# Linear attention with decay, then an MLP, on one core: the recurrence in chunks of 64 steps on column halves of the array instead of chunks of 128 on the whole array

## The chip, the cores and the metric

The kernel runs on one core of one Trainium2 chip. The metric is device time in microseconds (us) of one execution; lower is better. All arithmetic is in float32. The engines are called as in the profile: PE is TensorE's matmul, PEld its weight load, DVE is VectorE, ACT is ScalarE, POOL is GpSimd, SP is SyncE (here it only issues DMAs).

## What is computed

The reference is a recurrence over 768 steps for each of 4 batches and 8 heads, with 48 columns per head, followed by layer norm and a two-layer MLP with a residual:

```python
for t in range(S):
    kt, vt, rt, wt = (k[:, :, t], v[:, :, t], r[:, :, t], w[:, :, t])
    cur = np.einsum('bhd,bhe->bhde', u[None] * kt, vt)
    y[:, :, t] = np.einsum('bhd,bhde->bhe', rt, state + cur)
    state = wt[:, :, :, None] * state + np.einsum('bhd,bhe->bhde', kt, vt)
...
xn = (x - mu) / np.sqrt(var + 1e-06) * g_ln     # x: (4, 768, 384), the 8 heads side by side
ch = np.maximum(xn @ w_ch1, 0.0) @ w_ch2        # 384 -> 1536 -> 384
return x + ch
```

Here w lies between 0.8 and 0.95. The two MLP weights arrive as float64 and are converted to float32 on the chip.

## The kernel before

**Units.** A unit is one batch and one pair of heads, so there are 16 units, 4 to a batch. The two heads of a unit lie on 128 partitions, 64 each, of which 48 are used. The recurrence runs in 6 chunks of 128 steps. Inside a chunk the weight of step s in a later step t is a product of r, k and all decays between them; it is split by levels. At level `lev` the block size is n = 1, 2, .. 64, and an entry A[s, t] belongs to the level at which s lies in the left and t in the right of two sibling blocks. K and R are multiplied, level by level, by the products T of whole blocks of decays, so that A = K . R holds at each level.

**A level of a unit** (`levels`, 7 of them): PE makes 6 matmuls into two PSUM tiles of three chunks (line 269), with 128 columns of K as the stationary operand and 128 moving columns (two heads of 64). R is kept padded, as [128 partitions, 2 heads, 768], with zeros where the other head's partitions are, so that one matmul serves both heads. DVE copies the entries of this level out of PSUM through a mask, one copy for each three chunks (line 281); at the last level ACT does it (line 278). POOL multiplies K in place (line 282), and DVE multiplies R in place, one instruction per head on 64 partitions (line 293). K is read by this level's matmuls before POOL may change it, and R before DVE may.

**The rest of a unit.** `prep` turns w, k and r with PE transposes (line 210), copies them out with ACT (216, 220), makes the products T on POOL (232), and the step's own term on POOL and DVE (238 to 249). `tail` turns K back (310), makes the state that each chunk adds (`kv`, 5 matmuls, line 315), masks it (318), runs the recurrence over chunks on DVE (323, 325), and forms the output y from A and v (338) and from the carried state (343), which DVE adds into x (347).

**A matmul and its instructions.** A float32 matmul is two pairs of weight load and matmul on the chip: 672 matmuls at line 269 are 1344 instructions in the profile. A transpose is one pair.

**The MLP** (`mlp`) of a batch goes in two groups of 384 tokens: statistics and normalising on DVE, 9 transposes (381), 36 matmuls `h_ps` for the hidden layer (390), 36 `o_ps` for the output (400). It needs all four units of its batch.

**Order.** Python generators interleave one step of unit q's levels, the end of unit q - 1, the start of unit q + 1, one part of the weight conversion (24 parts, one per level step), and as many MLP steps of the batch before as keep pace. A scheduler in the framework then fixes each engine's order, so that an instruction can stand somewhat later or earlier than it was written. Each engine runs its own list in that order.

Of the kernel before, what the change touches and what calls it, by code (L numbers as in the profile page):

```python
# [28 lines left out]
def kernel(  # L29
# [26 lines left out]
    TT = 3                # token tiles that go through the MLP together  # L56
    RN = TT * P
    NG = NC // TT
    assert D <= HP and NC % CB == 0 and DM % P == 0 and DF % P == 0
# [3 lines left out]
    p3 = ctx.enter_context(tc.tile_pool(name="p3", bufs=3))  # L63
    ph = ctx.enter_context(tc.tile_pool(name="ph", bufs=14))
# [6 lines left out]
    NU = len(units)  # L71

    # a head's D columns lie in HP, the rest of which stays zero
# [4 lines left out]
    vs, xs = {}, {}  # L78
# [10 lines left out]
    def load_v(q):  # L89
        b, g = units[q]  # L90
        if g == 0:
            vs[b] = p2.tile([P, NC, H, D], F32, tag="v", name=f"v{b}")
        for h in (2 * g, 2 * g + 1):
            SP.dma_start(
                out=vs[b][:, :, h, :], in_=v[b, h].rearrange("(c p) d -> p c d", p=P)
            )

# [1 line left out]
    for nm in "wkr":  # L99
        for t in nat[nm]:  # L100
            POOL.memset(t[:, :, :, D:HP], 0.0)
# [372 lines left out]
```

## Time and profile before

| what | us |
|---|---|
| three runs | 804.66, 800.58, 804.47 (median 804.47) |
| span of the profiled execution, first to last instruction | 798.1 |
| PE busy | 704.1 (88%) |
| PEld busy | 527.0 (66%) |
| DVE busy | 457.0 (57%) |
| POOL busy | 258.8 (32%) |
| ACT busy | 191.5 (24%) |
| DMA, mean over the span | 42 GB/s |

The profiled execution shows its span only; what the runs' median has beyond it is 804.47 - 798.1 = 6.4 us. Busy time is the union of an engine's instructions; PE instructions overlap their neighbours' ends, so the pace of PE is read from the distance between starts and not from the duration of one. PEclk is the clock granted to TensorE, in tenths of full speed. In a group of instructions "128\*64" is the part of the array that is used, rows by columns; then come the output and input sizes.

### The profile page before, as it was taken

How to read it: one execution, taken by the hardware profiler on the slowest of the kernel's cores; microseconds unless marked ns; L12 is line 12 of the kernel's file. 1: busy time of each engine (PE TensorE's matmuls, PEld its weight loads, DVE VectorE, ACT ScalarE, POOL GpSimd, SP SyncE). 2: the span in 40 equal slices, each digit the busy share in tenths (PEclk: the TensorE clock that was granted, in tenths of full speed). 3: DMA queues.
4: the chain of work that ended last, by engine and by line, in shares of the span. 5: the costliest groups of instructions: out<-in, count | busy, mean ns of one | idle time of the engine just before them, and what ended most of it. 6: DMA issues, size and time to landing. Idle time of an engine off the chain costs nothing.

```text
span 798.1 us, 9669 instructions
## 1 busy us (share of the span) xinstructions
PE 704.1 (88%) x3640; PEld 527.0 (66%) x3640; DVE 457.0 (57%) x791; ACT 191.5 (24%) x402; POOL 258.8 (32%) x329
## 2 busy tenths in 40 slices
PE   4446665677699999999999999999999999999998
PEld 3346565567577767776867777777777776655554
DVE  5699999988964656485645555686444643200000
ACT  3034151503223122321322032212230212020110
POOL 8646564554532314141423333333121110000000
PEclk9558585859999999999999999999999999999999
DMA  9667241402310102023202020110000000000000
GB/s 155 102 139 154 64 120 60 119 5 46 75 30 16 41 20 46 0 55 70 56 1 46 21 55 1 30 35 11 1 1 11 20 1 1 20 11 11 20 1 30
DMA packets 107855, 33.86 MB, mean 42 GB/s; under 512 B 101536, under 2 KB 104736, under 8 KB 107808
## 3 DMA queue, kind: packets, MB, share of 16 engines
q1 hardware_dynamic: 107808, 33.24, 19.7%
q8 instruction: 29, 0.48, 0.2%
q14 instruction: 18, 0.15, 0.1%
HBM read 28.51 MB, written 4.72 MB: 42 GB/s over the span
## 4 chain that ended last, share of the span: by engine, by line
PE 76%; DVE 15%; POOL 3%; issue 3%; ACT 1%; DMA 1%; SPq 1%; POOLq 0%; ACTq 0%; DVEq 0%
PE h_ps L390 24%; PE o_ps L400 23%; PE a_ps L269 18%; DVE R L293 5%; PE y L338 4%; DVE A L281 3%; PE y L343 2%; POOL tot L232 2%; PE kv L315 1%; DVE we L184 1%; DVE wm L188 1%; PE k_ps L210 1%; DVE we L176 1%; PE r_ps L210 1%; DVE wm L192 1%
## 5 line engine op out<-in xcount | busy, mean ns | idle before, releaser
L269 PE MATMUL a_ps<-R,kT 128*128 128x128 f32 (+1 forms) x1344 | 198.5, 304 | 75.2 <-DVE R L293 64.5
L269 PEld LDWEIGHTS a_ps<-R,kT 128*128 128x128 f32 (+1 forms) x1344 | 186.2, 206 | 106.2 <-issue 44.1
L281 DVE COPY_PREDICATED A<-mask,a_ps 128x384 f32<-128x384 int8 x192 | 135.2, 730 | 139.1 <-PE a_ps L269 133.0
L390 PE MATMUL h_ps<-xT,w_sb 128*128 128x384 f32 x576 | 195.3, 489 | 0.5 <-ACT xT L382 0.5
L400 PE MATMUL o_ps<-w_sb,h 128*128 128x384 f32 x576 | 193.1, 487 | 0.0
L282 POOL TENSOR_TENSOR kT<-kT,tot 128x384 f32<-128x384 f32 x96 | 92.0, 958 | 257.4 <-PE a_ps L269 257.4
L400 PEld LDWEIGHTS o_ps<-w_sb,h 128*128 128x128 f32 x576 | 106.5, 190 | 67.1 <-issue 0.9
L390 PEld LDWEIGHTS h_ps<-xT,w_sb 128*128 128x128 f32 x576 | 105.6, 190 | 65.6 <-ACT xT L382 1.7
L293 DVE TENSOR_TENSOR R<-R,tot 64x384 f32<-64x384 f32 x160 | 133.4, 833 | 2.2
L406 DVE TENSOR_TENSOR o<-o_ps,x 128x384 f32<-128x384 f32 x24 | 13.4, 557 | 156.6 <-PE o_ps L400 156.6
L395 ACT ACTIVATE h<-h_ps 128x384 f32<-128x384 f32 x96 | 47.0, 490 | 149.1 <-PE h_ps L390 149.0
L338 PE MATMUL y<-v,A 128*128 128x48 f32 x384 | 56.0, 278 | 0.0
L338 PEld LDWEIGHTS y<-v,A 128*128 128x128 f32 x384 | 54.0, 207 | 0.5
L220 ACT COPY R<-r_ps 64x384 f32<-64x384 f32 x64 | 30.2, 472 | 55.3 <-PE r_ps L210 54.2
L292 ACT COPY rs<-R 64x384 f32<-64x384 f32 x32 | 16.3, 509 | 108.4 <-DVE R L293 107.9
L238 POOL TENSOR_TENSOR rk<-nat_k,nat_r 128x576 f32<-128x576 f32 x16 | 24.4, 1526 | 42.0 <-DMA nat_r<-in_r_dram 42.0
L343 PE MATMUL y<-s,rs 128*128 128x96 f32 x160 | 37.0, 316 | 0.0
L282 POOL TENSOR_TENSOR kT<-kT,wT 128x384 f32<-128x384 f32 x16 | 19.7, 1233 | 47.3 <-PE a_ps L269 47.3
L195 POOL TENSOR_TENSOR w_sb<-wm,we 128x384 f32<-128x384 f32 x24 | 27.8, 1157 | 20.4 <-DVE wm L192 14.4
L180 ACT ACTIVATE we<-we,bias 128x384 f32<-128x384 int32 x24 | 14.8, 615 | 71.3 <-DVE we L176 71.3
L232 POOL TENSOR_TENSOR tot<-tot 128x192 f32<-128x192 f32 (+4 forms) x80 | 29.4, 368 | 5.7
L343 PEld LDWEIGHTS y<-s,rs 128*128 128x128 f32 x160 | 27.2, 213 | 0.0
(59 smaller groups left out, 523.7 us busy)
## 6 DMA issues: line engine op xcount, KB each, us to landing
raw<-in_moe_w_ch_dram SPq DMA_DIRECT2D x24, 384.0 KB, 3.4
nat_w<-in_w_dram SPq DMA_DIRECT2D x32, 144.0 KB, 3.0
nat_k<-in_k_dram SPq DMA_DIRECT2D x32, 144.0 KB, 2.9
nat_r<-in_r_dram SPq DMA_DIRECT2D x32, 144.0 KB, 3.1
v<-in_v_dram SPq DMA_DIRECT2D x32, 144.0 KB, 3.6
out_dram<-o SPq DMA_DIRECT2D x24, 192.0 KB, 1.8
u_bc<-in_u_dram SPq DMA_DIRECT2D x1, 192.0 KB, 3.6
g_sb<-in_moe_g_ln_dram SPq DMA_DIRECT2D x1, 1.5 KB, 3.1
```

Of the source, the lines that this page charges most:

```text
L195: POOL.tensor_tensor(out=dst, in0=m, in1=e.bitcast(F32), op=ALU.mult)
L220: ACT.copy(out=a["r"][rows, j, cols], in_=ps[rows])
L232: POOL.tensor_tensor(out=t, in0=pair[:, :, 0], in1=pair[:, :, 1], op=ALU.mult)
L269: PE.matmul(ps[0:rows, c, :].rearrange("s (j q n) -> s j q n", j=2, n=n), a["k"][:, ds((c0 + c) * P, rows)], R[:, :, ds((c0 + c) * nq, nq) ...
L281: DVE.copy_predicated(out=to, mask=mask, data=ps)
L282: POOL.tensor_tensor(out=K[:, :, 0, :], in0=K[:, :, 0, :], in1=T[:, :, 1][:, :, None].broadcast_to([P, S // (2 * n), n]), op=ALU.mult,)
L293: DVE.tensor_tensor(out=rs[rows, :, 1, :] if last else R[rows, j, :, 1, :], in0=R[rows, j, :, 1, :], in1=T[rows, :, 0][:, :, None].broadca ...
L338: PE.matmul(y[:, i, ts(j, D)], a_bufs[q % 2][:, c, j, :], vs[b][:, c, 2 * g + j, :], start=i + j == 0, stop=c == 0, skip_group_check=True,)
L343: PE.matmul(y[:, i, :], a["rs"][:, ts(c, P)], s[:, c - 1, :], start=False, stop=True, skip_group_check=True,)
L390: PE.matmul(ps, w1_sb[:, kc, ts(f, P)], xT[:, kc, :], start=kc == 0, stop=kc == KC - 1,)
L395: ACT.activation(out=hs[f], in_=ps, func=AF.Relu)
L400: PE.matmul(ps, hs[f][:, ts(i, P)], w2_sb[:, f, :], start=f == 0, stop=f == FC - 1)
```

## The change

- **Chunks.** The recurrence has chunks of C = 64 steps (12 of them, `NM`) and 6 levels instead of 7. At each level a unit makes 12 matmuls of 64 stationary and 64 moving columns (two heads of 32). Even chunks write PSUM partitions 0 to 63 and odd chunks 64 to 127, which places them on the two column halves of the array. One PSUM bank holds a whole unit's level, and one masked DVE copy takes it out.
- **R unpadded.** R is [128, 768] without the zeros. DVE multiplies it in one instruction on 128 partitions. Only the half that the next level's matmuls need is copied by ACT, one copy per head, into one of four zeroed buffers (`pads`, two per unit of a pair). The multiplication of R therefore no longer waits for matmuls.
- **Two units at a time.** A round has units 2i and 2i + 1. `level` issues both units' matmuls, then both units' multiplications and pad copies, then both units' copies out of PSUM. There are 8 rounds and one more for the ends.
- **Ends.** `ends`, `states` and `outputs` of the two units of the round before are spread over levels 0 to 3. `states` makes one matmul per chunk pair and head (12 of them, 96 moving columns) and a recurrence of 11 steps of 48 columns; its result is padded by ACT. `outputs` makes 24 matmuls of 48 moving columns and 11 of 96. They use v in a zero-padded form that `load_vz` loads by DMA.
- **Weights and MLP.** Two parts of the weight conversion go with each level, so that the 24 parts are in the first two rounds. A batch's MLP is handed out at 1.05 times the pace of two rounds. ps_a has 2 banks instead of 3, ps_y 2 instead of 1.

The diff, cut to its core:

```diff
+    C = 64
+    NM = S // C
-    NLEV = 7
+    NLEV = 6
+    HALF = S // 2
-    ps_a = ctx.enter_context(tc.tile_pool(name="ps_a", bufs=3, space=PSUM))
-    ps_y = ctx.enter_context(tc.tile_pool(name="ps_y", bufs=1, space=PSUM))
+    ps_a = ctx.enter_context(tc.tile_pool(name="ps_a", bufs=2, space=PSUM))
+    ps_y = ctx.enter_context(tc.tile_pool(name="ps_y", bufs=2, space=PSUM))
...
+    pads = [const.tile([P, 2, HALF], F32, name=f"pad{i}") for i in range(4)]
+    a_bufs = [const.tile([P, NC, 2, C], F32, name=f"A{i}") for i in range(4)]
...
+    def right_half(q, lev):
+        n = 1 << lev
+        pad = pads[q % 2 * 2 + lev % 2]
+        R = st[q]["r"].rearrange("p (q two n) -> p q two n", two=2, n=n)
+        for j in range(2):
+            rows = ds(HP * j, HP)
+            ACT.copy(
+                out=pad[rows, j, :].rearrange("p (q n) -> p q n", n=n), in_=R[rows, :, 1, :]
+            )
+
+    def level(qs, lev):
...
+        for q in qs:
+            pad = pads[q % 2 * 2 + lev % 2]
+            ps = got[q] = ps_a.tile([P, NC, 2, C // 2], F32, tag="a", name=f"a_ps{q}_{lev}")
+            for c in range(NC):
+                for i in range(2):
+                    m = 2 * c + i
+                    PE.matmul(
+                        ps[ds(C * i, C), c], st[q]["k"][:, ts(m, C)], pad[:, :, ts(m, C // 2)],
+                        start=True, stop=True,
+                    )
+        for q in qs:
...
+            POOL.tensor_tensor(
+                out=K[:, :, 0, :], in0=K[:, :, 0, :],
+                in1=T[:, :, 1][:, :, None].broadcast_to(blocks), op=ALU.mult,
+            )
+            DVE.tensor_tensor(
+                out=R[:, :, 1, :], in0=R[:, :, 1, :],
+                in1=T[:, :, 0][:, :, None].broadcast_to(blocks), op=ALU.mult,
+            )
+            if not last:
+                right_half(q, lev + 1)
+        for q in qs:
...
+            if last:
+                for i in range(2):
+                    rows = ds(C * i, n)
+                    ACT.copy(out=A[rows, :, 0, 1, :], in_=ps[rows, :, 0, :])
+            else:
+                mask = masks[lev][:, None].broadcast_to([P, NC * 2, C // (2 * n), n])
+                DVE.copy_predicated(out=A[:, :, :, 1, :], mask=mask, data=ps)
...
+    def states(q):
...
+                for j in range(2):
+                    PE.matmul(
+                        kv[ds(HP * j, HP), i], a["kn"][:, c0 + i, ds(HP * j, HP)],
+                        vz[q % 2][:, c0 + i, :, j, :], start=True, stop=True,
+                    )
...
+                    DVE.scalar_tensor_tensor(
+                        out=s[:, m, :], in0=s[:, m - 1, :], scalar=a["T"][NLEV][:, m : m + 1],
+                        in1=new, op0=ALU.mult, op1=ALU.add,
+                    )
...
+    def outputs(q):
...
+                for j in range(2):
+                    for half in range(2):
+                        PE.matmul(
+                            y[ds(C * half, C), i, ts(j, D)], a_bufs[q % 4][:, c, j, :],
+                            vz[q % 2][:, c, half, j, :],
+                            start=i + j == 0, stop=c + half == 0, skip_group_check=True,
+                        )
+                for half in range(2):
+                    m = 2 * c + half
+                    if m:
+                        PE.matmul(
+                            y[ds(C * half, C), i, :], a["r"][:, ts(m, C)],
+                            a["s"][:, m - 1].rearrange("p j e -> p (j e)"),
+                            start=False, stop=True, skip_group_check=True,
+                        )
...
+    RATE = 1.05 * MLP_STEPS * 2 / (G * NLEV)
+    for rnd in range(NS + 1):
+        now, old, new = ([2 * i, 2 * i + 1] if 0 <= i < NS else [] for i in (rnd, rnd - 1, rnd + 1))
+        for lev in range(NLEV):
+            if now:
+                level(now, lev)
...
+            if lev == 3 and old and units[old[1]][1] == G - 1:
+                mlps.append(mlp(units[old[1]][0]))
+            mlp_steps(RATE / 2)
...
+            mlp_steps(RATE / 2)
+            next(ws, None)
+            next(ws, None)
```

How the order moves is shown at three places. In the rows below a name's first number is the level and, before the change, the first chunk; "x3" counts matmuls, and the sizes are output partitions by moving columns.

The first place is PE at level 2 while an MLP runs beside it (`h_ps` or `o_ps` is the MLP, `a_ps` the level, `y` the output of an earlier unit). Before:

```order
L390 MATMUL h_ps_1_0_2096<-xT_1_2032,w_sb 128x384 x3
L269 MATMUL a_ps_2_0_2102<-R_148,kT_1808 128x128 x3
L269 MATMUL a_ps_2_3_2107<-R_148,kT_1808 128x128 x3
L338 MATMUL y_0_2115<-v_736,A_145 128x48 x4
L343 MATMUL y_0_2115<-s_2064,rs_1970 128x96
L338 MATMUL y_0_2115<-v_736,A_145 128x48 x2
```

After the change, PE at level 2 of a later pair of units:

```order
L439 MATMUL o_ps_1_2_2841<-w_sb,h_1_3_2537 128x384
L439 MATMUL o_ps_1_2_2841<-w_sb,h_1_4_2543 128x384
L439 MATMUL o_ps_1_2_2841<-w_sb,h_1_5_2549 128x384
L295 MATMUL a_ps_2_2848<-pad_126,kT_2307 64x64 x12
L295 MATMUL a_ps_2_2861<-pad_128,kT_2318 64x64 x12
L375 MATMUL y_0_2884<-vz_91,A_132 64x48 x4
L383 MATMUL y_0_2884<-s_pad_134,rT_1803 64x96
```

Six matmuls on the whole array became twenty-four on column halves, those of two units in one stretch, and the output matmuls behind them are on column halves too.

The second place is DVE in the levels of the same time. Before, levels 2 and 3 of one unit (`R` is the multiplication, `A` the masked copy, `x` the addition of an output):

```order
L281 COPY_PREDICATED A_146<-mask_125,a_ps_2_0_2102 128x96x4
L281 COPY_PREDICATED A_146<-mask_125,a_ps_2_3_2107 128x96x4
L293 TENSOR_TENSOR R_148<-R_148,tot_1894 64x96x4 x2
L347 TENSOR_TENSOR x_1568<-y_0_2115,vo_1666 128x3x96
L281 COPY_PREDICATED A_146<-mask_129,a_ps_3_0_2149 128x48x8
L281 COPY_PREDICATED A_146<-mask_129,a_ps_3_3_2154 128x48x8
L293 TENSOR_TENSOR R_148<-R_148,tot_1894 64x48x8 x2
```

After the change, DVE around levels 0 and 1 of a pair of units:

```order
L324 COPY_PREDICATED A_130<-mask_150,a_ps_0_2649 128x384
L324 COPY_PREDICATED A_131<-mask_150,a_ps_0_2662 128x384
L309 TENSOR_TENSOR rT_2457<-rT_2457,tot_2157 128x96x4
L309 TENSOR_TENSOR rT_2468<-rT_2468,tot_2176 128x96x4
L445 TENSOR_TENSOR o_1_0_2709<-o_ps_1_0_2696,x_1014 128x384
L324 COPY_PREDICATED A_130<-mask_157,a_ps_1_2716 128x192x2
L324 COPY_PREDICATED A_131<-mask_157,a_ps_1_2729 128x192x2
```

A unit's level has one copy and one multiplication where it had two of each, and the multiplications of level 2 stand ahead of level 1's copies.

The third place is PE where the first MLP begins. Before, in the levels of unit 5 (`w_ps`, `k_ps` and `kn_ps` are transposes of the units' inputs, `xT_ps` those of the MLP, `kv` is a state):

```order
L269 MATMUL a_ps_1_3_1502<-R_148,kT_1309 128x128 x3
L315 MATMUL kv_1510<-v_736,kn_1458 128x96 x5
L210 MATMUL k_ps_0_1524<-ident,nat_k_81 128x128 x3
L381 MATMUL xT_ps_0_1_1539<-ident,xn_0_2_1484 128x128
L381 MATMUL xT_ps_0_2_1544<-ident,xn_0_0_1482 128x128
L381 MATMUL xT_ps_0_2_1544<-ident,xn_0_1_1483 128x128
L381 MATMUL xT_ps_0_2_1544<-ident,xn_0_2_1484 128x128
L269 MATMUL a_ps_2_0_1555<-R_148,kT_1309 128x128
L210 MATMUL k_ps_3_1529<-ident,nat_k_81 128x128 x3
L390 MATMUL h_ps_0_0_1549<-xT_0_1485,w_sb 128x384 x3
```

After the change, behind level 1 of units 6 and 7:

```order
L344 MATMUL kv_3_2114<-vz_91,kn_2031 64x96 x3
L333 MATMUL kn_ps_0_2129<-ident,kT_1093 128x128 x3
L420 MATMUL xT_ps_0_2_1798<-ident,xn_0_0_1773 128x128
L420 MATMUL xT_ps_0_2_1798<-ident,xn_0_1_1774 128x128
L420 MATMUL xT_ps_0_2_1798<-ident,xn_0_2_1775 128x128
L333 MATMUL kn_ps_3_2134<-ident,kT_1093 128x128
L429 MATMUL h_ps_0_0_1831<-xT_0_1776,w_sb 128x384 x3
L429 MATMUL h_ps_0_1_1837<-xT_0_1776,w_sb 128x384 x3
```

When PE reaches the first `h_ps`, five units' levels and two of unit 5's stand ahead of it before the change, and six units' levels and two levels of two more after it. In PE's list there are 33 stretches of one array shape before and 173 after, 106 of them behind the first `h_ps`.

More of the change, by code (lines that the diff above doesn't have):

```diff
@@ L77 @@
     }
-    vs, xs = {}, {}
+    vz = [const.tile([P, NC, 2, 2, D], F32, name=f"vz{i}") for i in range(2)]
+    vn, xs = {}, {}
     def load(q):
@@ L115 @@
     DVE.memset(eps, 1e-6)
+    pads = [const.tile([P, 2, HALF], F32, name=f"pad{i}") for i in range(4)]
+    a_bufs = [const.tile([P, NC, 2, C], F32, name=f"A{i}") for i in range(4)]
+    s_pads = [const.tile([P, NM - 1, 2, D], F32, name=f"s_pad{i}") for i in range(1)]
+    for t in (*pads, *a_bufs, *s_pads):
+        DVE.memset(t, 0.0)
+    for t in vz:
+        POOL.memset(t, 0.0)
     masks = []
@@ L247, in prep @@
         DVE.tensor_reduce(out=o, in_=rk, axis=AX.X, op=ALU.add)
[L248 removed]
+        a["vo"] = vn.pop(q)
         POOL.tensor_tensor(
[L250 to L263 removed]
+            out=a["vo"], in0=a["vo"], in1=o[:, :, :, None].broadcast_to([P, NC, 2, D]),
+            op=ALU.mult,
+        )
@@ L264, in levels @@
             K = a["k"].rearrange("p (q two n) -> p q two n", two=2, n=n)
             T = a["T"][lev].rearrange("p (q two) -> p q two", two=2)
[L266 to L281 removed]
+            blocks = [P, S // (2 * n), n]
@@ L442, with mlp_steps @@
-    for _ in mlps:
-        pass
+    for q in (0, 1):
+        for nm in "wkr":
+            turned(q, nm)
+        totals(q)
+    for q in (0, 1):
+        right_half(q, 0)
+        own_term(q)
+    load(2)
+    load(3)
+    mlps, owed = [], 0.0
+    def mlp_steps(n):
+        nonlocal owed
+        owed = owed + n if mlps else 0.0
+        while mlps and owed >= 1.0:
+            if next(mlps[0], mlps) is mlps:
+                mlps.pop(0)
+            else:
+                owed -= 1.0
+    RATE = 1.05 * MLP_STEPS * 2 / (G * NLEV)
@@ L447 @@
+    for m in mlps:
+        for _ in m:
+            pass
 _INS = ['r', 'k', 'v', 'w', 'u', 'moe_g_ln', 'moe_w_ch1', 'moe_w_ch2']
```

255 lines of the change are left out of this document (102 added, 153 removed).

## The prediction

> **What bounds the kernel now.** I read the profile's page first: the engines' busy shares and the span in 40 slices.
>
> ```profile
> span 798.1 us, 9669 instructions
> ...
> PE   4446665677699999999999999999999999999998
> ...
> DVE  5699999988964656485645555686444643200000
> ...
> PEclk9558585859999999999999999999999999999999
> ```
>
> There are two stages. In the first eleven slices PE is half busy and at a changing clock, and DVE is full for most of them; from then on PE is full to the end. The busy times by stage give the sizes. Its columns are the stage, its length, then PE, PEld, DVE, ACT and POOL busy with their instructions.
>
> ```profile
> 0.00:220.00 220.00, 134.13 (x787) 121.79 (x788) 191.93 (x324) 66.55 (x136) 126.19 (x165) 0.74 0.47 94
> 220.00:699.00 479.00, 475.20 (x2558) 349.66 (x2556) 260.57 (x460) 110.82 (x238) 132.60 (x164) 1.00 0.11 24
> 699.00:798.10 99.10, 94.79 (x298) 55.56 (x297) 4.51 (x9) 14.17 (x29) 0.00 (x0) 1.00 0.04 14
> ```
>
> Up to 220 us, where the first `h_ps` runs, DVE works 191.9 of 220 us. Behind that PE works 570.0 of 578.1 us. So the time is a start set mainly by DVE, and then a sum of PE's work. The timeline of PE gives the price of that work (start, duration, then the group; the distance between starts is the pace):
>
> ```profile
> 389.79 0.99 PE L338 MATMUL y<-v,A 128*128 128x48 f32 x8
> ...
> 391.55 0.82 PE L210 MATMUL r_ps<-ident,nat_r 128*128 128x128 f32 x6
> ...
> 404.63 4.04 PE L390 MATMUL h_ps<-xT,w_sb 128*128 128x384 f32 x12
> 408.50 1.50 PE L269 MATMUL a_ps<-R,kT 128*128 128x128 f32 x12
> 409.84 4.04 PE L390 MATMUL h_ps<-xT,w_sb 128*128 128x384 f32 x12
> 413.81 1.52 PE L269 MATMUL a_ps<-R,kT 128*64 128x128 f32 x12
> 415.26 4.14 PE L390 MATMUL h_ps<-xT,w_sb 128*128 128x384 f32 x12
> 419.23 1.52 PE L269 MATMUL a_ps<-R,kT 128*128 128x128 f32 x12
> ```
>
> - Twelve pairs with 384 moving columns take 408.50 - 404.63 = 3.87 us: 0.323 us a pair, 0.84 ns a column.
> - Twelve pairs with 128 columns take 409.84 - 408.50 = 1.34 us, 112 ns each, against 0.84 x 128 = 108 ns of streaming: the weight load of 128 columns lies hidden behind the stream.
> - Between the first row and the `r_ps` row lie sixteen output pairs (8 + 2 + 4 + 2) with 48 or 96 columns. They take 391.55 - 389.79 = 1.76 us, 110 ns each, though they stream for 40 or 81 ns. So a load of 128 columns costs some 110 ns of its own and sets the pace where the stream is shorter; that is 0.86 ns a column.
> - The last level uses 64 of the array's columns. Its twelve pairs take 1.45 us, 0.11 more than the other levels, and the intervals on both sides (409.84 to 413.81, 415.26 to 419.23) are 3.97 instead of 3.87. Going to another array shape and back costs 0.31 us.
>
> The end is MLP alone, from the chain of waits (start, length):
>
> ```profile
> 747.93 23.49 PE h_ps L390 x72
> 771.42 23.23 PE o_ps L400 x72
> ```
>
> A group of the MLP is 46.72 us; eight are 373.8 us, which the change doesn't touch. As a check of these prices on what lies behind 220 us: MLP 373.8; its 72 transposes 7.9; eleven units' levels (924 pairs), twelve units' ends (12 x 49 pairs) and ten units' transposes (180), 1692 pairs at 0.11, 186.1; eleven shape changes 3.4. That is 571.2 of 578.1 us; 7 us are gaps.
>
> **The start, step by step.** The groups by shape, with mean ns, for what DVE loses and gains, and for the copies and POOL work that change places:
>
> ```profile
> L293 DVE TENSOR_TENSOR R<-R,tot 64x384 f32<-64x384 f32 x160 | 133.4, 833 | 2.2
> L293 DVE TENSOR_TENSOR R<-R,wT 64x384 f32<-64x384 f32 x32 | 22.6, 707 | 0.4
> L293 DVE TENSOR_TENSOR rs<-R,tot 64x384 f32<-64x384 f32 x32 | 17.7, 553 | 0.9
> L281 DVE COPY_PREDICATED A<-mask,a_ps 128x384 f32<-128x384 int8 x192 | 135.2, 730 | 139.1 <-PE a_ps L269 133.0
> L318 DVE COPY_PREDICATED kv_sb<-own_head,kv 128x480 f32<-128x480 int8 x16 | 11.1, 695 | 10.3 <-PE kv L315 9.8
> L325 DVE SCALAR_TENSOR_TENSOR s<-s,decay,kv_sb 128x96 f32<-128x96 f32 x64 | 21.8, 340 | 1.6
> L247 DVE TENSOR_REDUCE own<-rk 128x12 f32<-128x576 f32 x16 | 12.0, 749 | 14.9 <-POOL vo L249 8.0 <-POOL rk L242 6.9
> L220 ACT COPY R<-r_ps 64x384 f32<-64x384 f32 x64 | 30.2, 472 | 55.3 <-PE r_ps L210 54.2
> L292 ACT COPY rs<-R 64x384 f32<-64x384 f32 x32 | 16.3, 509 | 108.4 <-DVE R L293 107.9
> L282 POOL TENSOR_TENSOR kT<-kT,tot 128x384 f32<-128x384 f32 x96 | 92.0, 958 | 257.4 <-PE a_ps L269 257.4
> L238 POOL TENSOR_TENSOR rk<-nat_k,nat_r 128x576 f32<-128x576 f32 x16 | 24.4, 1526 | 42.0 <-DMA nat_r<-in_r_dram 42.0
> L242 POOL TENSOR_TENSOR rk<-rk,u_bc 128x576 f32<-128x576 f32 x16 | 23.4, 1465 | 1.3
> L249 POOL TENSOR_TENSOR vo<-v,own 128x576 f32<-128x576 f32 x16 | 18.9, 1180 | 14.5 <-DVE x L347 14.4
> ```
>
> A unit's levels cost DVE (133.4 + 22.6 + 17.7 + 135.2) / 16 = 19.3 us before. Afterwards there are six multiplications, with as many elements per partition as one of the two had, and five copies: 6 x 0.833 + 5 x 0.730 = 8.65 us. Ahead of the first `h_ps` stand five units' levels now, 96.5 us; afterwards six units and two levels of units 6 and 7, which is 51.9 plus about 3.2 us. That saves 41.4. A tail costs 0.70 + 4 x 0.34 and a short copy, some 2.3 us; afterwards ten chained steps at most as long, 3.6 us; four tails add 5.4. Three more units have their own-term sums ready, 3 x 0.749 = 2.2. The net is -34 us, so DVE's 191.9 becomes 158. I keep the 28 us in which DVE waits now and put the first `h_ps` at 220 - 34 = **186 us**. The bounds are 175 (a third of the waiting goes as well, since R no longer waits for PE) and 205. The upper one is for POOL: its 126.2 us grow by two more units' preparation, 4.2 us each by the last three rows and their decay products besides, and three more multiplications of K at 0.958, to some 140. That is 75% of the shorter start, with K waiting for PE and PE for K in it. The weight conversion is unchanged in amount.
>
> What is costed at nothing there: the pad copies, 12 per unit at about 0.49 us against 4 copies of 0.472 and 2 of 0.509 removed, 3 us more per unit on ACT. ACT works 66.55 of the first 220 us, so it covers them; a pad copy waits for DVE's multiplication, and what is queued behind it on ACT is the MLP's `h` and the turned inputs. The rows on who waited for whom show that such a wait is harmless while PE is the bound (columns: total us, times, longest):
>
> ```profile
> ACT rs L292 <- DVE R L293: 107.9, 19, 17.4
> PE a_ps L269 <- DVE R L293: 64.5, 30, 7.3
> ```
>
> ACT waits 107.9 us for DVE today, and PE's gaps behind 220 us are still 8 us together (570.0 of 578.1). If that cover were gone, a level's burst would start up to two copies, 1 us, later, 48 bursts in all. The extra DMAs for the zero-padded v, 64 in all, queue on SP with the other loads and the stores of the output; the DMA engines are busy 11% of the middle stage, and I cost them at nothing too.
>
> **PE behind the start.** The order puts behind the first `h_ps`: 672 matmuls of levels, 288 of 48 columns and 132 of 96 for outputs, 132 of 96 for states, each two pairs, and 269 transposes at 0.11 us. With p for a pair of 64 loaded and 64 streamed columns, and one and a half times that for 96, the small ones are 1344 + 576 + 1.5 x 528 = 2712 p (a 48-column pair counts whole, for its load is as long). Terms in us: start 186; MLP 373.8; transposes 29.6; 106 changes of array shape, 53 pairs of them at 0.31, 16.4; gaps 13, the present 7 and about 6 more near the end, where the states' chain of ten DVE steps, 3.4 us, and the last outputs stand between the last `o_ps` and the last MLP. Sum: **618.8 + 2712 p**.
>
> No row shows p, since nothing runs on the second column half now. Its bounds from the rows above:
> - Both halves at once: a 64-column stream is 54 ns and a load 55 ns; halved, 28 ns. 618.8 + 75.9 = 694.7.
> - One after the other, loads hidden: 55 ns. 618.8 + 149.2 = 768.
> - Loads not hidden: 55 + 54 = 109 ns, or a pair costs 110 whatever its size: 618.8 + 296 = 915.
>
> Today's 798.1 is reached at p = 66 ns. I take 35 ns. The nearest row is the 1.34 us of `a_ps`: there load and stream overlap with only 4 ns a pair beyond the stream. For two halves that makes 27 + 4 = 31, and a few ns are added since both pairs of one float32 matmul stand behind each other on the same half, so that only neighbours from different matmuls overlap. Then 618.8 + 94.9 = 713.7, and with the 6.4 us that the median has beyond the span, **720 us**.
>
> The Trainium skill bears on this in "TensorEngine Tiling (Array Packing)", section Key Properties: different tiles can load weights and multiply in parallel, and changing the tiling mode drains the engine. The first would give p near 28; no run here shows it yet. With the second the trace agrees, by the 0.31 us.
>
> **The rivals.**
> 1. *The halves take turns.* One load path or one stream serves both halves, p = 55. For it: in the output rows the 110 ns pace is that of one load after another. Against: those loads all go to the same columns. 774 us, still faster, by the start (34 us) and one level less.
> 2. *Loads are not hidden on column halves* (slower). A half's load waits for the matmul that is running, p = 109. It acts at every small pair behind the start and decides from p = 66. 915 + 6 = 921 us. Against it stands the last level: twelve loads of 64 columns are hidden there behind 128-column streams (1.45 us, of which 1.29 is streaming). For it: never did a load for one half have to pass a running stream of another, nor was any pair in the trace paced faster than about 110 ns. "TensorE: Matmul & The Clock Gate", Part 3 of the Trainium skill, has a rule that speaks against the change: a load overlaps running matmuls only when it is in another row group, and both halves here use all rows. By that rule p would be the unhidden 109; the 1.34 us of `a_ps`, whole-array loads behind whole-array streams, already disagrees with it for one shape.
> 3. *The start doesn't shorten*: POOL's chain (K waits for PE, PE for K) or ACT takes DVE's place, and `h_ps` begins at 220 again. With p = 35 that is 720 + 34 = 754 us.
> 4. *It comes to nothing*: p of 64 to 67, from an issue cost per pair. 799 to 807 us.
>
> **Chances and range.** The overlap of both halves has 0.52, and its own range is 690 to 745; turns 0.26; unhidden loads 0.13; the unmoved start 0.06; nothing gained 0.03. A difference under 0.5% (4 us) can't be told from none. Faster: 0.52 + 0.26 + 0.06 = 0.84; same 0.03; slower 0.13. The range runs from p = 27 and a start at 178 (684 + 6 = 690) to turns with 58 ns and a start at 194 (784 + 6 = 790); it leaves out the slower rival and a little more.
>
> **What would show it.** In the changed trace: the 48 pairs of a level of both units in about 1.7 us with the MLP beside it (2.6 for turns, 5.2 for unhidden loads); the first `h_ps` at 175 to 205 us; DVE busy 158 us ahead of it; PE full from there on, with gaps near 13 us; the last two MLP groups unchanged at 46.7 us. I am wrong if PE idles between bursts behind the start, or if a level's burst takes over 3.2 us.

## The result, and the profile after

The changed kernel takes **707.06 us** (median of four runs, 706.58 to 707.64) against 802.77 (800.58 to 804.66) for the kernel before in the same call: ratio 0.8819, 95% interval [0.8793, 0.8844]. The forecast was 720 us, with a range from 690 to 790 and faster as the likeliest sign.

The page of the kernel after, with the strips of the same engines as before:

```profile
span 705.4 us, 13251 instructions
...
PE   5452373677899999999999999989999999799998
...
DVE  4779999897800532347044222573062013300000
...
PEclk9665865778999999999999999999999999999999
```

The picture is the same in kind: a start in which PE is half busy and DVE nearly full, then PE full to the end, with one dent near the end (the 7). A slice is now 17.6 us instead of 20. The busy times by stage, cut at the first `h_ps` and at the last MLP:

```profile
0.00:187.30 187.30, 106.39 (x1547) 89.64 (x1548) 157.36 (x284) 109.21 (x216) 144.75 (x179) 0.74 0.62 122
187.30:605.80 418.50, 408.73 (x3575) 272.07 (x3574) 149.84 (x343) 156.24 (x319) 99.21 (x124) 1.00 0.17 35
605.80:705.40 99.60, 95.57 (x298) 55.87 (x296) 4.60 (x9) 13.97 (x28) 0.00 (x0) 0.99 0.03 12
```

The start is 187.3 us long, with 157.36 us of DVE work. Behind it PE works 408.73 + 95.57 = 504.3 of 518.1 us, so its gaps are 13.8 us. The timeline of PE prices the new bursts (start, duration, then the group):

```profile
224.32 3.39 PE L439 MATMUL o_ps<-w_sb,h 128*128 128x384 f32 x10
227.64 1.62 PE L295 MATMUL a_ps<-pad,kT 128*64 128x64 f32 x48
229.09 0.44 PE L375 MATMUL y<-vz,A 128*64 128x48 f32 x9
...
241.72 1.46 PE L439 MATMUL o_ps<-w_sb,h 128*128 128x384 f32 x4
243.10 1.62 PE L295 MATMUL a_ps<-pad,kT 128*64 128x64 f32 x48
244.55 0.44 PE L375 MATMUL y<-vz,A 128*64 128x48 f32 x9
```

Both bursts of 48 pairs take 1.45 us from their start to that of the next group (229.09 - 227.64, 244.55 - 243.10): **30.2 ns a pair**. The change of shape ahead of them is seen as well: ten `o_ps` pairs at 0.323 us would take 3.23 us, and the next group starts after 3.32; four would take 1.29, and it starts after 1.38. So the way into the halves costs 0.09 us. The end, from the chain of waits:

```profile
655.25 23.49 PE h_ps L429 x72
678.74 23.23 PE o_ps L439 x72
```

It is what it was, 46.72 us for a group.

The parts of the 518.1 us behind the start: MLP 373.8, transposes 29.6 and gaps 13.8 leave 100.9 us for the small pairs and their shape changes. With the 16.4 us that the prediction put down for the changes, 84.5 us are left for its 2712 units of p, 31.2 ns each, near the 30.2 of the bursts.

What PE waits for between 187.3 and 605.8 us (total us, times, longest):

```profile
PE xT_ps L420 <- DVE xn L412: 3.5, 2, 3.1
PE kv L344 <- DVE x L388: 2.2, 4, 0.7
PE xT_ps L420 <- ACT xT L421: 1.2, 2, 0.6
PE kn_ps L333 <- POOL kT L305: 1.2, 1, 1.2
```

The 3.1 us are the dent near the end: DVE adds the last outputs, then makes the last batch's statistics and normalises, and nothing is left for PE. No wait for a pad copy stands among them.

### The profile page after: what moved, and what is told of

Its sections match the earlier page's. It is cut to its first block, busy times and chain, and to the rows that moved or that the text cites. A ratio compares the mean times of both kernels' runs of the same rounds, so it can differ in the third digit from the quotient of the medians.

```text
span 705.4 us, 13251 instructions
## 1 busy us (share of the span) xinstructions
PE 610.7 (87%) x5416; PEld 417.6 (59%) x5416; DVE 311.8 (44%) x635; ACT 279.4 (40%) x562; POOL 244.0 (35%) x303
## 4 chain that ended last, share of the span: by engine, by line
PE 69%; DVE 16%; POOL 8%; issue 3%; ACT 3%; POOLq 0%; DVEq 0%
PE h_ps L429 27%; PE o_ps L439 25%; PE a_ps L295 7%; DVE rT L309 3%; DVE wm L212 2%; PE kv L344 2%; DVE A L324 2%; DVE wm L216 2%; PE y L383 2%; POOL tot L249 2%; PE y L375 2%; DVE we L208 1%; PE xT_ps L420 1%; ACT pad L281 1%; DVE s L354 1%
## 5 line engine op out<-in xcount | busy, mean ns | idle before, releaser
L295 PE MATMUL a_ps<-pad,kT 128*64 128x64 f32 x2304 | 100.6, 242 | 51.9 <-DVE A L324 33.3
L281 ACT COPY pad<-rT 64x384 f32<-64x384 f32 x192 | 100.0, 521 | 88.9 <-PE a_ps L295 73.9
L295 PEld LDWEIGHTS a_ps<-pad,kT 128*64 128x64 f32 x2304 | 87.8, 153 | 75.8 <-issue 37.6
L324 DVE COPY_PREDICATED A<-mask,a_ps 128x384 f32<-128x384 int8 x80 | 59.1, 762 | 74.5 <-PE a_ps L295 73.5
L309 DVE TENSOR_TENSOR rT<-rT,tot 128x384 f32<-128x384 f32 x80 | 68.7, 870 | 28.9 <-ACT pad L281 28.4
L375 PE MATMUL y<-vz,A 128*64 128x48 f32 x768 | 44.3, 230 | 10.2 <-DVE s L354 10.1
L375 PEld LDWEIGHTS y<-vz,A 128*64 128x64 f32 x768 | 41.3, 148 | 13.5 <-issue 10.7
L354 DVE SCALAR_TENSOR_TENSOR s<-s,decay,kv 128x48 f32<-128x48 f32 x160 | 41.7, 261 | 4.8
L383 PE MATMUL y<-s_pad,rT 128*64 128x96 f32 x352 | 39.0, 268 | 0.9 <-ACT s_pad L361 0.9
L361 ACT COPY s_pad<-s 64x528 f32<-64x528 f32 x32 | 20.2, 630 | 45.9 <-DVE s L354 45.5
L383 PEld LDWEIGHTS y<-s_pad,rT 128*64 128x64 f32 x352 | 32.9, 148 | 1.2 <-ACT s_pad L361 1.2
```

What stands on the lines that cost most here:

```text
L281: ACT.copy(out=pad[rows, j, :].rearrange("p (q n) -> p q n", n=n), in_=R[rows, :, 1, :])
L295: PE.matmul(ps[ds(C * i, C), c], st[q]["k"][:, ts(m, C)], pad[:, :, ts(m, C // 2)], start=True, stop=True,)
L309: DVE.tensor_tensor(out=R[:, :, 1, :], in0=R[:, :, 1, :], in1=T[:, :, 0][:, :, None].broadcast_to(blocks), op=ALU.mult,)
L324: DVE.copy_predicated(out=A[:, :, :, 1, :], mask=mask, data=ps)
L354: DVE.scalar_tensor_tensor(out=s[:, m, :], in0=s[:, m - 1, :], scalar=a["T"][NLEV][:, m : m + 1], in1=new, op0=ALU.mult, op1=ALU.add,)
L375: PE.matmul(y[ds(C * half, C), i, ts(j, D)], a_bufs[q % 4][:, c, j, :], vz[q % 2][:, c, half, j, :], start=i + j == 0, stop=c + half == 0, ...
```

## The experiments

The theory after the result: both halves of the array run at once, in the levels, the states and the outputs alike, and DVE's work together with its waits sets the start. The rivals: a pair of 64 columns is cheap whatever its neighbours are, and two halves bring nothing by themselves; the gain comes from putting two units into one burst; the start is set by POOL or ACT and not by DVE. Each run was timed in several rounds beside the kernel before, which had a median of 802.2 us in the first call (first four runs), 800.55 in the second (three runs) and 801.18 in the third (two runs). A ratio is always to the kernel before; the stages are cut at each kernel's own first `h_ps`.

### One half after the other

The loops are exchanged in levels, states and outputs, so that neighbours in PE's list lie on the same half: at a level all twelve pairs of one half, then all twelve of the other.

```diff
-            for c in range(NC):
-                for i in range(2):
+            for i in range(2):
+                for c in range(NC):
                     m = 2 * c + i
...
-            for i in range(CB):
-                for j in range(2):
+            for j in range(2):
+                for i in range(CB):
...
-                for j in range(2):
-                    for half in range(2):
+            for half in range(2):
+                for i in range(CB):
+                    c = c0 + i
+                    for j in range(2):
```

> The same matmuls as the changed kernel (707.06 us), in an order in which neighbours stay on one column half: in a level first the six even chunks, then the six odd ones, and likewise in the states and the outputs. If the two halves work at once (my theory), that is lost here: a pair with 64 columns goes from 30 to about 55 ns, loads still hidden, the 48 pairs of a level take 2.7 instead of 1.45 us, and behind the first h_ps that makes 1344 x 25 ns for levels, 2.1 us for each of 12 units' outputs and 0.75 us for each of 11 units' states, 67 us together: about 774 us. If small pairs are simply cheap and nothing overlaps, the time stays at 707. If loads on one half are not hidden behind its streams, a pair takes 109 ns and the time is about 895.

Measured: 750.28 us, ratio 0.9354 [0.9334, 0.9374]. Its stages, and PE around one burst:

```profile
0.00:194.60 194.60, 125.69 (x1531) 110.90 (x1531) 154.60 (x280) 108.63 (x216) 139.34 (x178) 0.80 0.62 118
194.60:649.00 454.40, 450.00 (x3593) 314.13 (x3592) 151.07 (x350) 157.38 (x320) 100.65 (x126) 1.00 0.16 32
```

```profile
236.52 2.30 PE L295 MATMUL a_ps<-pad,kT 128*64 128x64 f32 x45
238.60 0.26 PE L374 MATMUL y<-vz,A 128*64 128x48 f32 x1
238.65 0.22 PE L295 MATMUL a_ps<-pad,kT 128*64 128x64 f32 x1
238.69 0.22 PE L374 MATMUL y<-vz,A 128*64 128x48 f32 x1
238.71 0.22 PE L295 MATMUL a_ps<-pad,kT 128*64 128x64 f32 x1
238.75 0.22 PE L374 MATMUL y<-vz,A 128*64 128x48 f32 x1
238.77 0.22 PE L295 MATMUL a_ps<-pad,kT 128*64 128x64 f32 x1
238.81 0.46 PE L374 MATMUL y<-vz,A 128*64 128x48 f32 x5
```

The same 48 pairs now take 238.77 - 236.52 = 2.25 us from the first start to the last, 48 ns each instead of 30, and PE works some 40 us more in the middle stage (450.00 - 408.73 = 41.3 by the rows; the cut lies 1.4 us into the last MLP here and 0.2 us in the kernel after). So side by side is where the gain lies. The rows at the seam say how. All 48 level pairs stand ahead of the outputs in PE's list, yet the first output pair starts at 238.60, while three level pairs are still to come. From then on level pairs (238.65, 238.71, 238.77) and output pairs (238.69, 238.75, 238.81) alternate: each half takes a pair every 0.06 us, and the two lists run independently. The single starts in the trace show the same at the three seams inside the burst, the first at 237.04 us: three pairs of the next half start early, and then each half goes on alone at 58 ns a pair. So PE looks some three pairs past a half that is occupied. This is also why the run came out below the 774 of the halves taking turns: 47 steps of 58 ns would be 2.73 us, and three seams inside the burst with three pairs each overlapped give 2.73 - 9 x 0.058 = 2.21, against 2.25 measured. The overlap was not switched off at the seams.

The run also prices the load. A pair on one half takes 58 to 60 ns (the five output pairs from 238.81 to the next group at 239.10 take 58 each), and 64 columns stream for 54 by 0.84 ns a column: the load lies hidden behind the stream of the pair ahead on the same half and the same rows.

The start is 7.3 us longer than in the kernel after (194.6 against 187.3), although DVE has 2.8 us less work in it and PE 19.3 us more. So PE's bursts, too, have a part in the length of the start.

### Two units apart

Each unit's level is issued by itself, with a third of the MLP steps in between.

```diff
-            if now:
-                level(now, lev)
+            for q in now:
+                level([q], lev)
+                if q % 2 == 0:
+                    mlp_steps(RATE / 3)
...
-            mlp_steps(RATE / 2)
+            mlp_steps(RATE / 3 if now else RATE / 2)
```

> The two units of a round have their levels one after the other with MLP work between them, not in one burst. PE's list then changes array shape 145 times behind the first h_ps instead of 106. If the price of that is the drain alone, 39 changes are 20 pairs at 0.31 us: +6 us, about 713. If the burst matters for more (waits between the engines' chains), +15 us or more. If a change of shape costs nothing when other work is queued, 707.

Measured: 706.21 us, ratio 0.8802 [0.8778, 0.8825], whose interval overlaps that of the kernel after.

```profile
0.00:186.50 186.50, 103.16 (x1533) 87.45 (x1533) 154.39 (x282) 108.90 (x217) 141.73 (x177) 0.76 0.63 123
186.50:606.00 419.50, 415.21 (x3591) 272.57 (x3590) 149.11 (x348) 156.34 (x319) 102.40 (x127) 1.00 0.17 35
```

Behind the first `h_ps` PE's list now changes shape 145 times instead of 106. PE's work in the middle stage rises by 415.21 - 408.73 = 6.5 us, against (39 / 2) x 0.31 = 6.0 by the price of a shape change. But the cut lies 1.4 us behind the last MLP's first `h_ps` here and 0.2 us in the kernel after, so 1.2 of the 6.5 us are the MLP's, and up to 0.9 are 14 more instructions that fall into the stage. Some 4.4 to 5.3 us are left for the shape changes: the price is about right, and rather high. But PE's gaps fall from 9.8 to 4.3 us, and the time stays. Two units in one burst is not what makes the change fast: it saves shape changes and gives the saving back in waits.

### R multiplied by two instructions

```diff
-            DVE.tensor_tensor(
-                out=R[:, :, 1, :], in0=R[:, :, 1, :],
-                in1=T[:, :, 0][:, :, None].broadcast_to(blocks), op=ALU.mult,
-            )
+            for j in range(2):
+                rows = ds(HP * j, HP)
+                DVE.tensor_tensor(
+                    out=R[rows, :, 1, :], in0=R[rows, :, 1, :],
+                    in1=T[rows, :, 0][:, :, None].broadcast_to([HP, S // (2 * n), n]), op=ALU.mult,
+                )
```

> R is multiplied by two DVE instructions of 64 partitions per unit and level, as before the change, all else as changed. That adds 39 instructions at 0.87 us to DVE ahead of the first h_ps. If DVE sets the start, the first h_ps moves from 187 us by most of 34 us, to 212 to 221, and the time is 732 to 741. If the chain over PE, POOL and ACT sets it and DVE has slack, less than 10 us are added. Behind the first h_ps nothing changes in either case.

Measured: 735.85 us, ratio 0.9172 [0.9144, 0.92].

```profile
0.00:214.50 214.50, 110.51 (x1541) 93.80 (x1541) 193.94 (x321) 108.39 (x217) 152.58 (x179) 0.73 0.55 107
214.50:634.00 419.50, 408.20 (x3579) 271.78 (x3575) 184.13 (x400) 154.33 (x316) 106.02 (x124) 1.00 0.17 35
```

DVE gets 36.6 us more work in the start, and the start is 27.2 us longer; in the middle stage DVE gets 34 us more, and all that lies behind the start is 3.1 us longer (735.7 - 214.5 = 521.2 against 518.1). The single multiplication on 128 partitions is thus worth 28.8 us, nearly all of it in the start. More DVE work lengthens the start by most of its amount, and behind the start it costs next to nothing.

### The pad copies twice

```diff
-            ACT.copy(
-                out=pad[rows, j, :].rearrange("p (q n) -> p q n", n=n), in_=R[rows, :, 1, :]
-            )
+            for _ in range(2):
+                ACT.copy(
+                    out=pad[rows, j, :].rearrange("p (q n) -> p q n", n=n), in_=R[rows, :, 1, :]
+                )
```

> Each pad copy on ACT is made twice, some 40 us more on ACT ahead of the first h_ps (109 of 187 us busy now) and 60 us behind it. The prediction costed the pad copies at nothing: 704 to 710 us. If each level of the start waits for its pad copies, one more microsecond for each of the 14 levels ahead of the first h_ps gives about 721; if ACT holds up the MLP's h behind it, more.

Measured: 716.37 us, ratio 0.893 [0.8905, 0.8955]; 9.3 us over the kernel after, and the intervals don't overlap.

```profile
0.00:185.10 185.10, 105.35 (x1447) 87.53 (x1448) 145.40 (x276) 141.30 (x280) 134.00 (x173) 0.70 0.62 124
185.10:615.00 429.90, 416.70 (x3675) 276.45 (x3674) 147.73 (x352) 221.97 (x448) 105.32 (x131) 0.99 0.17 34
```

ACT works some 98 us more in all, and a tenth of that shows. The start looks 2 us shorter, but 100 fewer PE instructions lie in it: the first `h_ps` now has 444 level matmuls ahead of it instead of 480. Work has moved behind it, and PE works 8.0 us more there (416.70 instead of 408.73). By the prices above the moved instructions are some 3.7 of these; the granted clock of the stage is 0.99 instead of 1.00, and the rest isn't split further by any run. PE's gaps there are 13.2 instead of 9.8 us. So ACT's share of the chain is not free to any amount. What the copies cost once, in the kernel after, this doesn't give; the waits of PE for a pad there say something of it (below).

### One DVE operation less in the weight conversion

```diff
             ACT.activation(out=m, in_=m.bitcast(I32), func=AF.Copy, bias=1.0, scale=2.0**-20)
-            DVE.scalar_tensor_tensor(
-                out=m, in0=lo, scalar=2.0**-52, in1=m, op0=ALU.mult, op1=ALU.add
-            )
```

> The weight conversion leaves out its last DVE step, which adds the low word of the float64 to the mantissa; the weights then have 20 bits of mantissa. That takes 24 instructions of 0.765 us, 18 us, off DVE ahead of the first h_ps and nothing behind it. If DVE sets the start, h_ps begins 14 to 18 us earlier and the time is 689 to 693 us; if the chain over PE, POOL and ACT is by now as long, it gives less than 7 us.

Measured: 697.17 us, ratio 0.8715 [0.8702, 0.8727].

```profile
0.00:174.90 174.90, 100.90 (x1529) 86.34 (x1530) 130.35 (x253) 108.70 (x216) 136.22 (x176) 0.77 0.67 131
```

In the same stage, the group of DVE with the longest idle time ahead of it (the last columns: idle us, and who ended it):

```profile
L264 DVE TENSOR_REDUCE own<-rk 128x12 f32<-128x576 f32 x8 | 6.0, 751 | 23.0 <-POOL rk L259 23.0
```

DVE loses 27 us of work in the start and the start loses 12.4: less than DVE's work, more than nothing. Of the 27 us, 18.4 are the removed instruction's own; most of the rest is that the instruction of line 212 (22.0 to 14.6 us) and the multiplication of R (32.7 to 28.0 us) got shorter. DVE is then busy 75% of it and waits 23.0 us for POOL's step of the own term alone (11.6 of its 12.7 there in the kernel after). So DVE's work doesn't set the start alone: as it shrinks, waits for POOL take over a part.

### Filling DVE's waits

Three runs tried to use this. The first loads the first six parts of the raw weights ahead of the third unit, so that DVE can convert while it waits; the second moves the last product of the conversion from POOL to DVE.

```diff
-        fetch(0)
+        for i in range(6):
+            fetch(i)
+        yield
...
         own_term(q)
+    next(ws)
     load(2)
```

> The first six parts of the raw weights are loaded ahead of units 2 and 3, some 14 us earlier. DVE, which converts its first part at 44 us in the changed kernel and idles about 8 us between 19 and 44 us, can fill those gaps: 5 to 8 us less, about 700. If units 2 and 3 then wait for their inputs, or if DVE's gaps are latencies that its list cannot fill, 707 or more.

```diff
-            POOL.tensor_tensor(out=dst, in0=m, in1=e.bitcast(F32), op=ALU.mult)
+            DVE.tensor_tensor(out=dst, in0=m, in1=e.bitcast(F32), op=ALU.mult)
```

> The last product of the weight conversion, 24 instructions of 1.21 us on POOL, is made on DVE. If only DVE's own work counts, DVE gets 24 x 0.6 to 0.87 us more ahead of the first h_ps: 14 to 21 us, 721 to 728. If POOL's instructions hold DVE's up (in the changed kernel's timeline the same 384-column DVE instruction takes 0.35 us alone and 1.15 beside a POOL instruction), DVE gets back 24 x 0.8 = 19 us: 702 to 709.

Measured: 707.04 us, ratio 0.8834 [0.8821, 0.8847], for the early loads, and 708.39 us, ratio 0.8857 [0.8839, 0.8875], for the product on DVE. Their starts, in this order:

```profile
0.00:186.09 186.09, 107.79 (x1548) 91.78 (x1548) 162.06 (x284) 108.18 (x216) 147.85 (x179) 0.74 0.64 123
```

```profile
0.00:187.69 187.69, 110.57 (x1545) 92.26 (x1546) 151.30 (x310) 108.55 (x217) 117.56 (x155) 0.75 0.63 122
```

Neither gains. With the early loads DVE's waits do shrink (186.09 - 162.06 = 24 us instead of 30), but its work grows by 4.7 us with the same instructions. With the product on DVE, 24 instructions of 0.635 us, 15.2 us in all, are added to DVE, and its work *falls* by 6.1. DVE's groups in the start of the kernel after and of the one with the product on DVE show where:

```profile
L309 DVE TENSOR_TENSOR rT<-rT,tot 128x384 f32<-128x384 f32 x33 | 32.7, 1000 | 2.2 <-ACT pad L281 2.1
...
L212 DVE TENSOR_SCALAR wm<-raw 128x384 int32<-128x384 int32 x24 | 22.0, 917 | 0.0
```

```profile
L309 DVE TENSOR_TENSOR rT<-rT,tot 128x384 f32<-128x384 f32 x34 | 27.1, 803 | 2.2 <-ACT pad L281 2.2
L219 DVE TENSOR_TENSOR w_sb<-wm,we 128x384 f32<-128x384 f32 x24 | 15.2, 635 | 0.0
L212 DVE TENSOR_SCALAR wm<-raw 128x384 int32<-128x384 int32 x24 | 14.3, 597 | 0.0
```

The same instruction takes 917 ns with POOL's products beside it and 597 without them (the last section shows single ones). DVE's busy time in the start is partly time in which POOL held it up. That it went down and the start did not says that DVE's waits took over. The third run has both edits:

> The two edits that fill DVE's start together: the first six raw weight parts are loaded early, and the product of the weight conversion is on DVE instead of POOL. Alone, the first put the first h_ps at 186.1 us with DVE busy 162.1 us, the second at 187.7 us with DVE busy 151.3 us. Theory 1, DVE's work and its contention with POOL set the start: with POOL's 29 us of products gone and DVE's early waits filled, DVE has some 151 to 156 us of work and waits 24 us or less, so the first h_ps comes at 175 to 180 us and the median falls to 695 to 701 us. Theory 2, a chain sets it (a level's copies, multiplication of R, pad copy, burst, multiplication of K, round after round) and DVE's waits only move: the first h_ps stays at 185 to 188 us and the median at 704 to 708 us.

Measured: 709.09 us, ratio 0.8856 [0.883, 0.8881]. Its start, and the longest waits in it (total us, times, longest):

```profile
0.00:187.82 187.82, 111.19 (x1534) 94.47 (x1534) 160.21 (x304) 107.56 (x216) 117.35 (x154) 0.75 0.61 122
```

```profile
POOL kT L308 <- PE a_ps L298: 57.8, 18, 23.7
ACT pad L284 <- DVE rT L312: 24.0, 11, 5.1
...
PE a_ps L298 <- DVE A L327: 14.0, 6, 5.5
...
PE a_ps L298 <- ACT pad L284: 13.1, 6, 5.7
```

The theory of work and contention on DVE alone falls: POOL has 27 us less to do, DVE's waits fall only to 27.6 us, and the start stays. What is left is a chain of a level: POOL's K waits for PE's burst, ACT's pad for DVE's R, PE's next burst for the pad and for A. The conversion's instructions stand in DVE's list between R and A. In the kernel after, DVE multiplies R at 42.80 us and makes the next masked copy only at 63.66, with little but conversion between them, and PE stands idle for 18.7 us ahead of the burst at 64.35:

```profile
PE a_ps L295 <- DVE A L324: 33.3, 4, 18.7
```

The early loads break that wait up (5.5 us is the longest for A above), and the time goes into other links. So DVE's work lengthens the chain, as the runs with more and with less of it show, but to move it about in these ways didn't shorten it. Which link binds most isn't settled by these runs: none put a level's copies ahead of the conversion, and none gave the levels a third PSUM bank, so that a burst need not wait for the copies of the one before.

### Early loads, product on DVE and units apart

This joins the last three edits that came out even, since the units apart had lowered PE's gaps and could loosen the chain of the start.

> The kernel of the run with both start edits, and also each unit's level called by itself with a third of the MLP steps between. Alone, that last edit left the first h_ps where it was (186.5 us) and the median at 706 us, with 6.5 us more PE work and 5.5 us less of PE's gaps. If the parts add, the time is that of the other run within 2 us. If two units apart loosen a chain in the start (one unit's DVE work beside the other's burst), the first h_ps comes 3 us or more earlier than in the other run.

Measured: 703.36 us (702.33 to 704.04), ratio 0.8778 [0.8758, 0.8798], 5.7 us under the run with the two edits.

```profile
0.00:184.24 184.24, 109.92 (x1548) 91.76 (x1548) 160.69 (x307) 108.00 (x216) 119.46 (x155) 0.78 0.62 124
184.24:601.00 416.76, 412.43 (x3575) 271.02 (x3574) 146.07 (x344) 156.04 (x319) 99.10 (x125) 1.00 0.17 35
```

The start is 3.6 us shorter than with the two edits alone, and all behind it 3.2 us (516.4 against 519.6), where gaps of 4.3 us stand in place of 9.7 and PE's work is some 3 us more. PE's granted clock in the start is 0.78 against 0.75, but that alone doesn't make the difference: of the single runs, those at a mean clock of 0.932 took 703.55 us here and 707.54 and more there. So to issue the units apart does loosen the chain of the start a little, as one unit's DVE work can go beside the other's burst; no run shows that link by itself. It is the fastest version with the whole computation, by about half a per cent over the kernel after, and the intervals of the two just overlap.

## Why the prediction was right, step by step

- **The start: right, in part by luck.** 186 us forecast, 187.3 measured; DVE's work in it 158 against 157.4; its waits were kept at 28 and are 30. But the terms of DVE's work miss, and their misses cancel. The levels were to save 41.4 us and saved 45.9 (109.9 us up to 220 us before, 64.0 in the start after): the 96.5 us taken for before leave out the two levels of unit 5, and R's multiplication, taken at 0.833 us, took 1.00 after the change. The state steps cost 0.7 us more and not 5.4, the own-term sums 0.7 and not 2.2. And the weight conversion, held to be unchanged, grew by 11.3 us with the same 120 DVE instructions, from 68.1 to 79.4. Its instruction that takes 22.0 us after the change (line 212, above) took before:

```profile
L188 DVE TENSOR_SCALAR wm<-raw 128x384 int32<-128x384 int32 x24 | 16.3, 680 | 0.0
```

With POOL's products moved to DVE these same 120 instructions take 65.5 us. So the growth goes with POOL's products beside them, a term that the prediction put at nothing. The two experiments that add or take DVE work in the start confirm the mechanism in sign (27 us later with 36.6 more, 12.4 earlier with 27 less), but not that the waits would stay as they are: a part of any saving turns into waiting for POOL. The waits were carried over and not worked out, so their agreement is luck as well.
- **Gaps: right in sum.** 13 forecast, 13.8 measured. The gap near the end is there, 3.1 us and 0.6 behind it instead of about 6, and what makes it is the last batch's statistics and normalising rather than the state's chain; some 2 us more are spread over the middle stage.
- **MLP and shape changes: right.** 46.72 us for a group; 4.4 to 5.3 us for 39 more shape changes where 0.31 a pair of them gives 6.0. The transposes' 29.6 us were not measured by themselves.
- **The pair p: the mis-sized term.** 35 ns taken, 30.2 in the bursts and 31.2 over all. Pairs and shape changes together were 94.9 + 16.4 = 111.3 us and came out at 100.9. The step that failed is the addition of "a few ns" because "both pairs of one float32 matmul stand behind each other on the same half, so that only neighbours from different matmuls overlap". The runs show that a half's list doesn't stop for the other's: each half takes a pair every 58 to 60 ns by itself, with PE some three pairs ahead, so that both passes of a matmul overlap with the other half's, and p is just half of 60. Without those few ns the text had 31.
- **The rest of the miss.** The start is 1.3 us over, the gaps 0.8, the pairs 10.4 under: 8.3 us of span. The median lies 707.06 - 705.4 = 1.7 us beyond the span and not 6.4: 4.7 more. That is the 13.0 us between 720 and 707.06. The 6.4 set the span of one execution against the median of runs that differ by 4 us; in the runs with both on record, each time is 1.7 to 1.8 us beyond that run's own span.
- **Costed at nothing: the pad copies.** In the start of the kernel after, PE's idle time ahead of the level bursts names a pad for 4.4 of its 51.3 us:

```profile
L295 PE MATMUL a_ps<-pad,kT 128*64 128x64 f32 x960 | 50.6, 266 | 51.3 <-DVE A L324 33.3 <-POOL kT L305 8.0 <-ACT pad L281 4.4
```

So by this row they cost some 4.4 us there directly, and behind the start no wait for them is among PE's. The cover is thin, though, as the doubled copies showed with 9.3 us.
- **Rival 1, turns (774): fell.** A burst takes 1.45 us and not 2.6. Had the halves taken turns, their order would not matter; with the halves apart the same burst takes 2.25.
- **Rival 2, unhidden loads (921): fell.** A pair takes 58 to 60 ns even on a single half, not 109. The rule named there, "TensorE: Matmul & The Clock Gate", Part 3 of the Trainium skill, that a load overlaps running matmuls only in another row group, disagrees with the trace: both halves use all rows, and loads are hidden behind the same half's stream. The other rule of that part of the Trainium skill, that matmuls start in the order of the program, disagrees as well: an output pair starts at 238.60 us, ahead of the level pairs at 238.65 to 238.77 that stand before it. The Trainium skill's "TensorEngine Tiling (Array Packing)", Key Properties, that tiles load and multiply in parallel, agrees, with 30 ns against 58 to 60.
- **Rival 3, the start doesn't shorten (754): fell**, with 187.3 against 220 us. A chain of POOL, PE and ACT exists all the same, with DVE in it: by the waits above it is what kept the later edits from shortening the start further.
- **Rival 4, nothing gained: fell.**

## What to carry to other kernels

Where a float32 matmul uses 64 columns, write neighbours to opposite column halves: the two halves run as two lists of their own, here at 58 to 60 ns a pair each for 64 moving columns, and it is the neighbours in the program that must differ, since PE looked only some three pairs ahead. Price such a change as a sum (start, pairs, shape changes, gaps) from the rows of the kernel before, with the pace of a pair taken from its streaming. And where an engine is full in a start, look whether its instructions are longer beside another engine's: taking 27 us off POOL shortened DVE's instructions, and the start still didn't move, because its waits had a chain of their own. A sum that comes out can hide terms that cancel: check each term against the trace, and not the total alone.

## What the runs showed of the hardware

**PE's two halves keep their own order.** With the halves apart, pairs of one half start ahead of pairs of the other that stand before them in the program, some three pairs early (238.60 us against 238.65 to 238.77 above).

**A DVE instruction is held up by POOL's.** The timeline of the kernel after, DVE first and then POOL:

```profile
49.40 1.15 DVE L212 TENSOR_SCALAR wm<-raw 128x384 int32<-128x384 int32 x1
...
51.20 0.35 DVE L212 TENSOR_SCALAR wm<-raw 128x384 int32<-128x384 int32 x1
...
52.21 1.15 DVE L212 TENSOR_SCALAR wm<-raw 128x384 int32<-128x384 int32 x1
```

```profile
49.28 1.04 POOL L219 TENSOR_TENSOR w_sb<-wm,we 128x384 f32<-128x384 f32 x1 [1.23 <-DVE wm L216]
52.10 1.04 POOL L219 TENSOR_TENSOR w_sb<-wm,we 128x384 f32<-128x384 f32 x1 [1.77 <-DVE wm L216]
```

The instruction of line 212 takes 0.35 us at 51.20, with POOL idle from 50.32 to 52.10, and 1.15 us at 49.40 and 52.21, where a product of POOL began 0.11 to 0.12 us earlier; both times it ends 0.23 us or less after POOL's. It looks like waiting for the other's end rather than like running at a lower rate. "SBUF — State Buffer" of the Trainium skill, section "Who interferes with whom", has a port pair that DVE and GpSimd share as an exclusive lock, and the trace agrees with that: 0.80 us of a POOL instruction of 1.04 are added to a DVE instruction of 0.35.
